# Inverses of decay products: a reciprocal of every token in place of a forward scan

## The chip, the cores and the metric

The kernel runs on one core of a Trainium2 chip. The metric is the device time of one execution in microseconds (us), the median of several runs. The engines are called TensorE (PE, its weight loads PEld), VectorE (DVE), ScalarE (ACT), GpSimd (POOL) and SyncE (SP, which issues most transfers). They work side by side and wait for one another by semaphores; each engine takes its own instructions in the order of the program.

## The reference

A gated linear attention is followed by a two-layer block with a SoLU activation and a layer norm:

```
q, k, v, alpha: (batch 4, heads 8, tokens 768, head_dim 48), alpha in 0.8 to 1.0
for t in range(S):
    state = alpha[:, :, t, :, None] * state + k_t (outer) v_t
    y[:, :, t] = q_t @ state
x = y as (3072 tokens, 384)
h = x @ w_in                       # 384 -> 1024
solu = h * softmax(h)
ln = (solu - mean) / sqrt(var + 1e-6) * g_ln
out = ln @ w_out                   # 1024 -> 384
```

## The kernel before, in words

**The attention in chunks.** The 768 tokens are six chunks g = 0 to 5 of 128. A recurrence with a decay can be computed by matmuls within a chunk, if every key is multiplied by the product of the decays after it and every query is divided by the product of the decays after it. Then the score of a key s for a query t carries just the decays between s and t. So each chunk needs two arrays with features on the partitions and tokens along the free axis:

- `hT`, the product of alpha from each token to the end of the chunk. `scan_back` makes it with a scan from the last token to the first (L220). The view `hk` of the same memory is shifted by one token, so that column t holds the product of the decays behind t.
- the inverse of it, which is written into `aT`, in place of alpha. `scan_on` makes it.

Four batches of 32 features lie on the 128 partitions, for 8 heads; the 48 features of a head are cut into 32 and 16, and the ends of two heads share a block. So there are 12 blocks of 128 tokens, which are worked on in three parts of four blocks (`i` = 0, 1, 2; part 2 holds the ends). Each block has one column more than tokens (516 columns to a part), in which a scan finds the start value of the next block.

**How `scan_on` makes the inverse before.** For a part it takes the product of the whole chunk (column 1 of each block, 4 numbers to a partition), bounds it from below by 1e-13 (`least`, L234), takes its reciprocal (L235) into the first column of `seed`, and runs one forward scan over alpha (L236, recorded at the line of the helper, L220): each step multiplies by the next alpha. For part 2 it first copies the chunk's products of all 12 blocks to `fend` (L231), from which a check at the end of the kernel tells whether this fast path may stand or a general path has to run.

**Who uses it.** `keys` multiplies kT by hk (GpSimd L244; VectorE L685 and L762 in chunks 0 and 1). `queries` multiplies the transposed q by aT (GpSimd L255; VectorE L693, L772, L780 in chunks 0 and 1), `apart` (ScalarE L248) spreads the ends of two heads over two blocks of qv, and `scores` (TensorE L282) needs both. `masked` (VectorE L293) applies the causal mask, `read_state` and `read_values` (TensorE L314) make y, `next_state` (L364, L374) brings the state forward.

**The two-layer block and the order of the work.** Stage g is the two-layer block of chunk g: eight steps s, each with an `up` of six matmuls (L389) into one of two banks h, an exp on ScalarE (e, L403), the product h*e on VectorE (L404, which frees the bank), a square on ScalarE (u, L405), sums over steps (`running`, L420, one on GpSimd and one on VectorE), and half a `down` (eight matmuls, L500) of the chunk before. `finish` (L517 to L533) turns the sums of a block of rows into a factor r on GpSimd (L530) and scales the output on ScalarE (o_sb, L532).

The order is written out by hand. The attention of chunk g + 1 is spread over the steps of stage g by a table:

```python
        behind={0: "states v keys", 1: "load on2 on0 on1", 2: "lasts firsts", 3: "apart", 5: "decay", 6: "alpha", 7: "back"},
```

"on2 on0 on1" are the three calls of `scan_on`, behind the up of step 1; "lasts firsts" are the transposes of q on VectorE (L198, L195) with the `queries` behind them on GpSimd; "apart" follows in step 3 and "scores0" at the end of step 4. Chunks 0 and 1 and most of chunk 2 are done ahead of these stages in a straight line of code (L673 to L809), where VectorE also converts the weights, which arrive as 64-bit floats, to 32-bit ones (L594 to L606). There the order is, for chunk 1:

```python
    scan_on(1, 2)
    nc.vector.tensor_tensor(out=qe, in0=tq[2], in1=aT[:, H:NB, 1:SW], op=ALU.mult)
    apart()
    finish(0)
    decay(1)
    in_range(7)
    for i in range(2):
        scan_on(1, i)
        part = slice(NP * i, NP * i + NP)
        nc.vector.tensor_tensor(out=qv[:, part], in0=tq[i], in1=aT[:, part, 1:SW], op=ALU.mult)
    down(2, 0)
    scores(1, 0)
```

Of the kernel before, what the change touches and what calls it, by code (L numbers as in the profile page):

```python
# [9 lines left out]
FP = mybir.dt.float32  # L10
# [4 lines left out]
ALU = mybir.AluOpType  # L15
AX = mybir.AxisListType
P = 128
# [15 lines left out]
def fast_path(ctx, tc, q, k, v, alpha, moe_w_in, moe_w_out, moe_g_ln, out):  # L33
# [12 lines left out]
    nc = tc.nc  # L46
# [5 lines left out]
    NP = H // 2  # L52
# [6 lines left out]
    LEAST = 1e-13  # L59
    PS = bass.MemoryType.PSUM  # L60

    def pool(name, bufs, **kw):
        return ctx.enter_context(tc.tile_pool(name=name, bufs=bufs, **kw))

    const = pool("const", 1)
# [3 lines left out]
    small = pool("small", 4)  # L69
# [27 lines left out]
    fend = const.tile([P, G, NB], FP, name="fend")  # L97
# [19 lines left out]

    SW = P + 1
    aT = const.tile([P, NB, SW], FP, name="aT")
    seed = [const.tile([P, NP, SW], FP, name=f"seed{i}") for i in range(2)]  # L120
    unit = const.tile([P, NP, SW], FP, name="unit")
    hT = const.tile([P, NB * SW + 2], FP, name="hT")
    h4 = hT[:, 0 : NB * SW].rearrange("p (j s) -> p j s", s=SW)

    hk = hT[:, 2 : NB * SW + 2].rearrange("p (j s) -> p j s", s=SW)[:, :, 0:P]
# [90 lines left out]
    def scan(out, data, start, flip):  # L216
        a, o, s = (x.rearrange("p j s -> p (j s)") for x in (data, out, start))
        if flip:
            a, o, s = a[:, ::-1], o[:, ::-1], s[:, ::-1]
        nc.vector.tensor_tensor_scan(out=o, data0=a, data1=s, initial=1.0, op0=ALU.mult, op1=ALU.add)  # L220
# [5 lines left out]

    def scan_on(g, i):
        part = slice(NP * i, NP * i + NP)
        s = seed[i % 2]
        if i == 2:  # L230
            nc.vector.tensor_copy(out=fend[:, g], in_=h4[:, :, 1])  # L231

        least = small.tile([P, NP, 1], FP, name="least")
        nc.vector.tensor_scalar(out=least, in0=h4[:, part, 1:2], scalar1=LEAST, scalar2=None, op0=ALU.max)  # L234
        nc.vector.reciprocal(out=s[:, :, 0:1], in_=least)  # L235
        scan(aT[:, part], aT[:, part], s, False)  # L236

    def keys_T(g):
        firsts(kn, kT[:, 0:H])
# [414 lines left out]
    nc.gpsimd.memset(unit[:, :, 0:1], 1.0)  # L654
    nc.gpsimd.memset(aT[:, :, 0:1], 0.0)
    nc.gpsimd.memset(hT[:, NB * SW : NB * SW + 2], 1.0)
    for s in seed:
        nc.gpsimd.memset(s, 0.0)
    nc.gpsimd.memset(state, 0.0)
    load_v_first(0)  # L660
    fetch(0, 3, 2)
# [18 lines left out]
    turned(kn, ends_of(kn), t)  # L680
    alpha_over(0)
    scan_on(0, 2)
    for i in range(3):
        part = slice(NP * i, NP * i + NP)
        nc.vector.tensor_tensor(out=kT[:, part], in0=t[i], in1=hk[:, part], op=ALU.mult)  # L685
    scan_on(0, 0)
    t = three("tp_q", [(ps_o, "o"), (ps_o, "o"), (ps_a, "a0")])
    turned(qn, ends_of(qn), t)
    for i in (2, 0, 1):
        if i == 1:  # L690
            scan_on(0, i)
        part = slice(NP * i, NP * i + NP)
        nc.vector.tensor_tensor(  # L693
            out=qe if i == 2 else qv[:, part], in0=t[i], in1=aT[:, part, 1:SW], op=ALU.mult
        )
        if i == 2:
            apart()
# [61 lines left out]
    for i in range(3):  # L759
        scan_back(1, i)  # L760
        part = slice(NP * i, NP * i + NP)
# [15 lines left out]
# [3 lines that stand above are left out]
# [150 lines left out]
    def compare(out, x, bound, op):  # L930
# [6 lines left out]
        out=chunks[:, :, 2], in0=sums[:, :, 2], scalar=0.25, in1=sums[:, :, 3], op0=ALU.mult, op1=ALU.is_le  # L937
# [6 lines left out]
    else:  # L944
# [9 lines left out]
        out=bad, in0=all_ok[0:1, 0:1], scalar1=float(P * ends[-1]), scalar2=None, op0=ALU.is_lt  # L954
# [415 lines left out]
def kernel(tc, *args):  # L1370

    with ExitStack() as ctx:
        taken = fast_path(ctx, tc, *args)
    with tc.If(taken > 0):
        general_path(tc, *args)
# [30 lines left out]
```

## Time and profile before

The median of three runs is 393.45 us (390.79 to 393.57). The profiled execution spans 388.2 us.

| engine | busy us | share of the span | instructions |
|---|---|---|---|
| TensorE, matmuls | 369.6 | 95% | 4661 |
| TensorE, weight loads | 223.5 | 58% | 4661 |
| VectorE | 250.6 | 65% | 417 |
| ScalarE | 144.0 | 37% | 252 |
| GpSimd | 124.9 | 32% | 135 |

A group of instructions is given by its line, engine, operation, what it writes and reads with shapes, how many there are, then their busy time in us and the mean of one in ns, then the idle time of the engine ahead of them and what ended it. A row of slices cuts the span into 40 equal parts; a digit is the busy share of a slice in tenths. The chain that ended last is followed back from the last instruction, at each step to what released it or to the one before on its engine; a line of it, and of the timeline, begins with the start and the length in us.

### The profile page before, as it was taken

To read this page: it belongs to the slowest core of one execution; us is meant where nothing else is said; L and a number is where in the kernel's file an instruction comes from. 1 tells how busy PE (TensorE), PEld (TensorE's weight loads), DVE (VectorE), ACT (ScalarE), POOL (GpSimd) and SP (SyncE) were. 2 spreads that over 40 slices of the span, in tenths; PEclk is the share of its full clock that TensorE was granted. 3 is DMA by queue.
4 is the path that set the end of the run, shared out by engine and by line. 5 is a ranking of instruction groups with operands and counts; after the bars stand their busy time and mean duration, and the time that the engine had idled before them with its cause. 6 is when DMAs were issued, how large, how long until landed. Compare 5 with 4: busy or idle time off the path is not lost.

```text
span 388.2 us, 10598 instructions
## 1 busy us (share of the span) xinstructions
PE 369.6 (95%) x4661; PEld 223.5 (58%) x4661; DVE 250.6 (65%) x417; ACT 144.0 (37%) x252; POOL 124.9 (32%) x135
## 2 busy tenths in 40 slices
PE   8798999887999999999999999999999999999995
PEld 8685345455665556656566556566555675555552
DVE  0989888996989766793755893665895511444410
ACT  2627775554425425225152224253123231333111
POOL 4020000032032992436413536422634620333210
PEclk9989999999999999999999999999999999999999
DMA  9956989402357300774000863000600000000011
GB/s 186 193 154 173 243 256 179 104 20 69 95 128 102 83 4 2 100 167 102 22 3 22 133 141 95 22 3 24 101 0 22 22 24 2 20 21 21 22 43 48
DMA packets 86567, 30.79 MB, mean 79 GB/s; under 512 B 68072, under 2 KB 84720, under 8 KB 86512
## 3 DMA queue, kind: packets, MB, share of 16 engines
q1 hardware_dynamic: 85488, 29.11, 34.7%
q10 hardware_dynamic: 1024, 0.92, 0.7%
q8 instruction: 38, 0.62, 0.7%
q14 instruction: 17, 0.14, 0.1%
HBM read 25.30 MB, written 4.72 MB: 77 GB/s over the span
## 4 chain that ended last, share of the span: by engine, by line
PE 71%; DVE 12%; SPq 6%; ACT 4%; DMA 3%; issue 2%; DVEq 0%
PE o L500 29%; PE h L389 24%; PE y L314 9%; PE a L282 5%; SPq L564 3%; SPq L152 2%; DMA room<-in_moe_w_in_dram 2%; DVE room L404 2%; PE kv L364 1%; ACT sq L581 1%; DVE aT L220 1%; DMA kn<-in_k_dram 1%; DVE low L605 1%; DVE top L597 1%; DVE sT L293 1%
## 5 line engine op out<-in xcount | busy, mean ns | idle before, releaser
L500 PE MATMUL o<-w_out,room 128*128 128x385 f32 x384 | 133.5, 491 | 1.1 <-DVE least L234 1.1
L389 PE MATMUL h<-x,w_in 128*128 128x512 f32 x288 | 132.2, 598 | 1.8 <-DVE g_col L618 1.8
L500 PEld LDWEIGHTS o<-w_out,room 128*128 128x128 f32 x384 | 71.3, 190 | 57.3 <-issue 15.4
L389 PEld LDWEIGHTS h<-x,w_in 128*128 128x128 f32 x288 | 53.0, 189 | 60.5 <-issue 48.4
L404 DVE TENSOR_TENSOR room<-h,e 128x512 f32<-128x512 f32 x40 | 27.7, 692 | 81.3 <-ACT e L403 81.1
L403 ACT ACTIVATE e<-h 128x512 f32<-128x512 f32 x40 | 23.9, 598 | 103.6 <-PE h L389 103.6
L530 POOL TENSOR_TENSOR r<-sums,mhalf 128x1 f32<-128x1 f32 x20 | 14.3, 714 | 139.4 <-DVE sums L522 139.4
L420 POOL TENSOR_TENSOR p<-p,e 128x512 f32<-128x512 f32 x30 | 41.7, 1390 | 15.8 <-ACT e L403 15.7
L405 ACT ACTIVATE u<-room 128x512 f32<-128x512 f32 x40 | 25.2, 630 | 42.2 <-DVE room L404 42.2
L293 DVE TENSOR_TENSOR sT<-a,mask 128x512 f32<-128x512 f32 x44 | 27.3, 682 | 10.0 <-PE a L282 8.9
L282 PE MATMUL a<-qv,kT 32*128 32x128 f32 x704 | 27.6, 289 | 4.4 <-DVE least L234 2.1
L282 PEld LDWEIGHTS a<-qv,kT 32*128 32x128 f32 x704 | 24.1, 196 | 11.9 <-issue 4.2
L220 DVE TENSOR_TENSOR_SCAN hT<-aT,unit 128x516 f32<-128x516 f32 x18 | 23.1, 1339 | 8.7 <-ACT aT L677 8.6
L420 DVE TENSOR_TENSOR p<-p,u 128x512 f32<-128x512 f32 x30 | 23.1, 771 | 6.5 <-ACT u L405 6.5
L244 POOL TENSOR_TENSOR kT<-kT,hT 128x1024 f32<-128x1024 f32 (+1 forms) x8 | 13.3, 1676 | 43.2 <-DVE kT L195 43.2
L314 PE MATMUL y<-sT,vn 128*32 128x128 f32 x768 | 23.6, 274 | 1.6 <-issue 0.9
L220 DVE TENSOR_TENSOR_SCAN aT<-aT,seed 128x516 f32<-128x516 f32 x18 | 23.0, 1278 | 0.6
L314 PEld LDWEIGHTS y<-sT,vn 128*32 128x32 f32 x768 | 20.9, 110 | 3.7 <-issue 2.7
L212 ACT ACTIVATE sq<-an,mone 128x1536 uint8<-128x1536 f32 x12 | 18.8, 1569 | 0.2
L314 PE MATMUL y<-qv,state 32*32 32x128 f32 x960 | 16.8, 277 | 1.0 <-DVE sT L293 0.9
L314 PEld LDWEIGHTS y<-qv,state 32*32 32x32 f32 x960 | 12.1, 103 | 7.9 <-issue 4.8
L532 ACT ACTIVATE o_sb<-o,r 128x384 f32<-128x384 f32 x16 | 9.3, 581 | 18.8 <-POOL r L530 18.8
(141 smaller groups left out, 378.2 us busy)
## 6 DMA issues: line engine op xcount, KB each, us to landing
an<-in_alpha_dram SPq DMA_DIRECT2D x20, 192.0 KB, 5.0
out_dram<-o_sb SPq DMA_DIRECT2D x20, 192.0 KB, 1.9
room<-in_moe_w_out_dram SPq DMA_DIRECT2D x8, 384.0 KB, 4.8
kn<-in_k_dram SPq DMA_DIRECT2D x16, 192.0 KB, 4.0
qn<-in_q_dram SPq DMA_DIRECT2D x16, 192.0 KB, 3.8
vn<-in_v_dram SPq DMA_DIRECT2D x10, 256.0 KB, 4.0
room<-in_moe_w_in_dram SPq DMA_DIRECT2D x16, 128.0 KB, 3.7
kn<-in_k_dram SPq DMA_DIRECT2D x4, 384.0 KB, 5.7
```

The source lines that it names most:

```text
L212: nc.scalar.activation(out=sq, in_=x, func=AF.Relu, scale=sign, bias=mone, accum_out=over[:, g, i : i + 1])
L220: nc.vector.tensor_tensor_scan(out=o, data0=a, data1=s, initial=1.0, op0=ALU.mult, op1=ALU.add)
L282: nc.tensor.matmul(a[b][:, i], lhsT=kT[quarter(b), kb], rhs=qv[quarter(b), qb], start=kb == h, stop=kb != h, tile_position=(32 * b, 0), sk ...
L293: nc.vector.tensor_tensor(out=sT[:, b, half * NP : half * NP + NP], in0=a[b], in1=mask[:, None, :].to_broadcast([P, NP, P]), op=ALU.mult,)
L314: nc.tensor.matmul(y_bank(b)[quarter(r), a], lhsT=lhsT, rhs=rhs, start=(b, r) not in begun, stop=stop, tile_position=(row, 32 * r), skip_g ...
L389: nc.tensor.matmul(h, lhsT=w_in[:, a, f * P : (f + 1) * P], rhs=d["x"][:, a].rearrange("p b t -> p (b t)"), start=(a == 0), stop=(a == KC ...
L403: nc.scalar.activation(out=e, in_=h, func=AF.Exp)
L404: nc.vector.tensor_tensor(out=u, in0=h, in1=e, op=ALU.mult)
L405: nc.scalar.activation(out=u2, in_=u, func=AF.Square)
L420: eng.tensor_tensor(out=p, in0=d[0][i] if f == 1 else p, in1=d[f][i], op=ALU.add)
L500: nc.tensor.matmul(d["o"][:, 0 : DM + 1], lhsT=u_of(g, f)[:, b * P : b * P + P], rhs=w_out[:, f], start=(f == 0), stop=(f == FC - 1), skip ...
L530: nc.gpsimd.tensor_tensor(out=r, in0=s[:, 3:4], in1=mhalf, op=ALU.pow)
```

## The change

The inverse of each part is taken directly: one reciprocal on VectorE of the 512 products in `hk`, written to the columns of `aT` where the scan wrote its result. With it go the bound from below, the reciprocal of four numbers, the forward scan and the `seed` tiles with their memsets at the start. The copy of the chunk's products to `fend` moves from VectorE to ScalarE. It is meant to get the same array with one instruction per part in place of three dependent ones.

```diff
-    seed = [const.tile([P, NP, SW], FP, name=f"seed{i}") for i in range(2)]
...
     def scan_on(g, i):
         part = slice(NP * i, NP * i + NP)
-        s = seed[i % 2]
         if i == 2:
-            nc.vector.tensor_copy(out=fend[:, g], in_=h4[:, :, 1])
-
-        least = small.tile([P, NP, 1], FP, name="least")
-        nc.vector.tensor_scalar(out=least, in0=h4[:, part, 1:2], scalar1=LEAST, scalar2=None, op0=ALU.max)
-        nc.vector.reciprocal(out=s[:, :, 0:1], in_=least)
-        scan(aT[:, part], aT[:, part], s, False)
+            nc.scalar.copy(out=fend[:, g], in_=h4[:, :, 1])
+
+        nc.vector.reciprocal(out=aT[:, part, 1:SW], in_=hk[:, part])
...
-    for s in seed:
-        nc.gpsimd.memset(s, 0.0)
```

## The prediction

> **What bounds the kernel now.** I read the totals of the page first, then the slices, then the costliest groups and VectorE's own groups, then the chain that ended last in order of time, then the timeline around the changed instructions.
>
> ```profile
> PE 369.6 (95%) x4661; PEld 223.5 (58%) x4661; DVE 250.6 (65%) x417; ACT 144.0 (37%) x252; POOL 124.9 (32%) x135
> ...
> DVE  0989888996989766793755893665895511444410
> ...
> L220 DVE TENSOR_TENSOR_SCAN aT<-aT,seed 128x516 f32<-128x516 f32 x18 | 23.0, 1278 | 0.6
> L234 DVE TENSOR_SCALAR least<-hT 128x4 f32<-128x4 f32 x18 | 6.5, 362 | 0.0
> L235 DVE RECIPROCAL seed<-least 128x4 f32<-128x4 f32 x18 | 3.2, 180 | 0.8
> L231 DVE COPY fend<-hT 128x12 f32<-128x12 f32 x6 | 2.5, 409 | 0.0
> ```
>
> TensorE (PE) is busy 95% of the span, but this averages two regimes. In the row of slices (9.7 us each) VectorE (DVE) is almost full for the first ten, then at five to nine tenths. The chain agrees: until 89 us it is made of DMA, ScalarE and VectorE pieces, from about 134 us of matmuls end to end. So VectorE's load counts nearly one for one early, and later only where it outgrows what TensorE's work hides. The last four lines are all that the change takes from VectorE: 35.2 us. The chain in order of time (start, length, what) shows the early regime for chunk 1:
>
> ```profile
> 84.66 1.34 DVE aT L220
> 86.03 0.69 DVE qv L780
> 87.12 1.30 DVE aT L220
> 88.45 0.70 DVE qv L780
> 89.19 2.06 PE a L282 x62
> ```
>
> Scan, multiply, scan, multiply, and only then may TensorE make the scores. The timeline of VectorE in a late stage (chunk 4, start, length) shows what one inverse costs from start to start:
>
> ```profile
> 221.43 0.17 DVE L231 COPY fend<-hT 128x12 f32<-128x12 f32 x1
> 221.51 0.16 DVE L234 TENSOR_SCALAR least<-hT 128x4 f32<-128x4 f32 x1
> 221.71 0.18 DVE L235 RECIPROCAL seed<-least 128x4 f32<-128x4 f32 x1
> 221.93 1.23 DVE L220 TENSOR_TENSOR_SCAN aT<-aT,seed 128x516 f32<-128x516 f32 x1
> 223.08 1.17 DVE L234 TENSOR_SCALAR least<-hT 128x4 f32<-128x4 f32 x1
> ...
> 227.18 0.67 DVE L420 TENSOR_TENSOR p<-u,u 128x512 f32<-128x512 f32 x1
> ```
>
> Three inverses fill 221.43 to 227.18, that is 5.75 us.
>
> [...] The trace has only reciprocals of 4 elements: 180 ns, where other 4-element operations (L464, L466) take 166. [...] the copy of fend took 1.61 us at 108.92, beside GpSimd's L244. The reciprocals stay within 180 to 181 ns[...].
>
> **The price of the new instruction.** It is one reciprocal of 128x512 per third of a chunk, 18 in all; no row has it. [...] *Fast end:* all the excess over a plain operation is a fixed cost, [...] about 0.69 us, like the 128x512 multiply L404 (692 ns). *Slow end:* [...] **4.41 us**. *Between:* [...] 2.96 us. I take 4.41[...]; it is an estimate.
>
> **The change part by part, at 4.41 us.**
> VectorE's busy time becomes 250.6 - 35.2 + 18 x 4.41 = 294.8 us. What of this reaches the end:
>
> - *Chunk 0 (13 to 22 us).* Its three inverses now take 1.80 (fend to scan end, 13.17 to 14.97), 1.64 and 1.71 us: 5.15. They become 13.2, so the last qv is 8.1 us later. VectorE then idled 1.16 us before the masking at 23.0; that idle goes, as the first scores are done earlier relative to it. Behind the masking VectorE converts weights (L594 to L606) with hardly a gap until 37 us, and the first products of stage 0 wait for those. **+7.0**.
> - *Chunk 1 (80 to 90 us).* 80.83 to 82.55, 84.24 to 86.0 and 86.63 to 88.41, with finish(0) between: 5.3 us become 13.2. All lies on the chain shown. **+7.9**.
> - *Chunk 2.* Parts 2 and 0 run from 108.92 to 114.19, 5.27 us[...], and become 8.82: +3.55. Behind them on VectorE's queue is finish(3), for whose factor ScalarE's output waits, and behind that on ScalarE the exp of stage 1. Those products thus start later, and TensorE's third up waits for a free h bank. Part 1, 119.27 to 121.40, 2.13 us, becomes 4.41: +2.28. The transposes of q, GpSimd's queries and scores(2,0) follow; TensorE already waits 0.30 and 0.33 us there. **+5.8**.
> - *Chunks 3, 4, 5 (stages 2 to 4, slot s = 1).* 5.75 us become 13.2, +7.45. Queued behind on VectorE: running(1), the product h*e of s = 2, the transposes of q. The first wait is up(4), scheduled at 233.78 in the stage shown: it needs the h bank that the product of s = 2 frees at 228.45 + 7.45 = 235.9, 2.1 us late. The second wait is longer and contains the first: transposes, then GpSimd's queries and p, then r, then ScalarE's o_sb, then apart, which now ends at 238.14 and would end at 245.6, where TensorE wants scores at 239.04. That is +6.55, the same in stage 2 (180.75 against 181.58), and +7.3 in stage 4, where scores start at 294.75 just as apart works. **+20.4**. TensorE runs these stages without gaps, so nothing is won back.
> - *Copy of fend on ScalarE.* A copy of about 0.2 us, six times, of values long made; ScalarE idles by 1 us and more around slot 1 (2.2 us before e at 224.97). **0**. Fewer memsets on GpSimd at 3 us: it then waits 15.7 us for v. **0**.
>
> Sum: 7.0 + 7.9 + 5.8 + 20.4 = 41.1; 393.45 + 41.1 is about **434.5 us**.
>
> **The rivals.**
> *B[...] (2.96 us and up).* Three inverses take 8.88 us. Chunk 0: +3.7 - 1.1 = +2.6; chunk 1: +3.6; chunk 2: 5.92 - 5.27 plus 2.96 - 2.13 = +1.5; stages: 3.1 - 0.9 of slack = 2.2 twice and 3.0 once, +7.4. Sum +15.1, **408.5 us**. [...]
> *C[...] faster than before.* Three inverses take 2.1 us. Chunk 0: up to -3.1, of which I count -2, as the weights' transfers end the next wait; chunk 1: 5.3 to 2.1, -3.2; chunk 2: about -1, what TensorE waits there; later nothing, since matmuls follow without gaps. Sum -6.2, **387 us**. For it: [...] that fixed parts of small operations differ (COPY L462 of 8 elements takes 172 ns). [...]
> *D[...].* [...] the 1.74 us of an inverse now: **no change**, 393 us.
>
> **How the numbers follow.** Forecast 0.52, B 0.22, C 0.20, D 0.06. The range goes from C, 386, to 444, the forecast with a quarter more on its 41 us for queues that I have not followed; it leaves out about half of C and a tenth of the forecast. Faster by over 1%: 0.20; within 1%: 0.06; slower: 0.74.
>
> **What would show it.** Right: a group RECIPROCAL aT<-hT 128x512 x18 near 4.4 us each; VectorE busy near 295 us; the chain passing through that line in chunks 0 to 2; waits of TensorE for apart's qv ahead of scores in stages 2 to 4; the late chain no longer matmuls alone. Wrong: a reciprocal below 2 us, which puts C or D in its place; or one of 4.4 us with matmuls still end to end after 134 us, which would mean that the queue behind slot 1 has more slack than I read.

## The result

The changed kernel takes 418.8 us (median; 416.0 to 421.5) against 392.9 us before: the ratio is 1.067, with a 95% interval of 1.056 to 1.077. It is slower by about 26 us. The forecast was 434.5 us: the side was right, the size was not.

The page of the changed kernel, its totals, its slices (40 of 10.5 us), the clock that TensorE was granted, and the costliest group of VectorE:

```profile
PE 383.5 (91%) x4661; PEld 233.2 (56%) x4661; DVE 275.6 (66%) x375; ACT 144.3 (34%) x258; POOL 119.6 (28%) x133
...
DVE  1999879995797877695465596465696531344420
...
PEclk9969999986899999999699999899999899999999
...
L231 DVE RECIPROCAL aT<-hT 128x512 f32<-128x512 f32 x18 | 59.2, 3322 | 0.1
```

One reciprocal takes 3.3 us. Eighteen of them put 59.2 us on VectorE where 35.2 us went. ScalarE is busy as long as before (144.3 us, 144.0 before), GpSimd 5 us less (119.6, 124.9 before). But TensorE's busy time grew by 14 us with the same 4661 matmuls: some of them ran more slowly, and the clock row dips to 6 and 8 tenths in single slices.

A late stage of it, chunk 3, on VectorE (start, length):

```profile
176.67 0.69 DVE L399 TENSOR_TENSOR room<-h,e 128x512 f32<-128x512 f32 x1 [1.71 <-ACT e L398]
...
177.73 9.77 DVE L231 RECIPROCAL aT<-hT 128x512 f32<-128x512 f32 x3
187.42 0.63 DVE L415 TENSOR_TENSOR p<-u,u 128x512 f32<-128x512 f32 x1
187.96 0.68 DVE L399 TENSOR_TENSOR room<-h,e 128x512 f32<-128x512 f32 x1
188.56 1.14 DVE L197 STREAM_TRANSPOSE qe<-qn 128x512 f32<-128x512 f32 x1
```

The three inverses fill 9.7 us instead of 5.75; the product and the transposes of q stand behind them. The chain that ended last, in the same stage (start, length, what):

```profile
189.78 1.18 POOL qe L250
...
191.67 2.62 POOL qv L250 x2
...
195.99 0.56 POOL r L525
...
196.57 0.58 ACT o_sb L527
197.15 1.22 ACT qv L243 x2
198.37 0.48 ACT kg L298
...
198.99 4.67 PE a L277 x64
203.65 2.60 PE h L384 x3
```

This is the second wait that the prediction named: queries on GpSimd, then its r, then o_sb and apart on ScalarE. Behind apart the three copies kg still follow, and it is for them that TensorE waits (3.64 us until the copy of L298 ends), since the scores go into the banks that they read. TensorE then runs the 64 score matmuls of chunk 3 in 4.67 us, which took 2.72 us in the trace of before:

```profile
181.58 2.72 PE L282 MATMUL a<-qv,kT 32*128 32x128 f32 x64
```

**Where the time came from.** The start of the product h*e of a given step marks how far a kernel is. Its delay against before, read from the timelines (us), with what the runs below give; "again" is a second execution of the changed kernel (run after_again):

| stage, step | changed | again | late | early | spread | filler15 | filler_both |
|---|---|---|---|---|---|---|---|
| 0, 0 | 3.3 | 3.1 | 1.3 | 2.7 | 3.2 | 3.1 | 2.6 |
| 1, 2 | 13.9 | 11.7 | 3.9 | 11.3 | 13.2 | 11.7 | 10.7 |
| 2, 0 | 13.7 | 11.5 | 3.8 | 11.1 | 14.5 | 11.4 | 10.2 |
| 3, 0 | 20.3 | 17.2 | 9.2 | 11.2 | 15.3 | 15.3 | 13.7 |
| 4, 0 | 25.9 | 23.5 | 15.9 | 11.2 | 16.5 | 19.8 | 17.6 |
| 5, 0 | 31.2 | 27.1 | 22.1 | 11.2 | 19.1 | 24.0 | 21.4 |

The changed kernel loses 13.7 us before stage 2 and 6.6, 5.6 and 5.3 us in stages 2 to 4; in stage 5, which has no attention, nothing. These are single executions: the one profiled of the changed kernel is its longest (421.5 us) and that of before one of its shorter ones (390.2), so 31 us stand here for the 26 of the medians. The second execution of the changed kernel (417.4 us) is 27.1 us late at the end. "late" has the early code of before unchanged and still shows 3.9 us at stage 1, of which 1.7 are eight matmuls of down that took 4.55 us in place of 2.86. So a few microseconds lie within what the same code does.

### The profile page after: what moved, and what is told of

The parts are those of the page before. It is cut to its first block, busy times and chain, and to the rows that moved or that the text cites. A ratio compares the mean times of both kernels' runs of the same rounds, so it can differ in the third digit from the quotient of the medians.

```text
span 419.5 us, 10560 instructions
## 1 busy us (share of the span) xinstructions
PE 383.5 (91%) x4661; PEld 233.2 (56%) x4661; DVE 275.6 (66%) x375; ACT 144.3 (34%) x258; POOL 119.6 (28%) x133
## 4 chain that ended last, share of the span: by engine, by line
PE 55%; DVE 22%; issue 7%; ACT 7%; POOL 4%; DMA 3%; SPq 0%; DVEq 0%; ACTq 0%; POOLq 0%
PE o L495 20%; PE h L384 17%; PE y L309 9%; DVE aT L231 8%; PE a L277 6%; DVE room L399 2%; DMA an<-in_alpha_dram 2%; POOL qv L250 2%; DVE hT L219 2%; ACT sq L576 1%; DMA kn<-in_k_dram 1%; DVE sT L288 1%; DVE qe L197 1%; ACT qv L243 1%; PE kv L359 1%
## 5 line engine op out<-in xcount | busy, mean ns | idle before, releaser
L495 PE MATMUL o<-w_out,room 128*128 128x385 f32 x384 | 138.0, 505 | 2.7 <-DVE o_mean L521 2.7
L384 PE MATMUL h<-x,w_in 128*128 128x512 f32 x288 | 134.0, 605 | 1.2 <-DVE g_col L613 1.2
L495 PEld LDWEIGHTS o<-w_out,room 128*128 128x128 f32 x384 | 73.6, 196 | 61.2 <-issue 21.4
L231 DVE RECIPROCAL aT<-hT 128x512 f32<-128x512 f32 x18 | 59.2, 3322 | 0.1
L277 PE MATMUL a<-qv,kT 32*128 32x128 f32 x704 | 34.9, 340 | 20.3 <-ACT kg L298 7.2
L277 PEld LDWEIGHTS a<-qv,kT 32*128 32x128 f32 x704 | 30.9, 241 | 28.1 <-issue 15.3
L288 DVE TENSOR_TENSOR sT<-a,mask 128x512 f32<-128x512 f32 x44 | 27.3, 681 | 13.5 <-PE a L277 13.5
```

The lines of the kernel that those rows point to most:

```text
L231: nc.vector.reciprocal(out=aT[:, part, 1:SW], in_=hk[:, part])
L277: nc.tensor.matmul(a[b][:, i], lhsT=kT[quarter(b), kb], rhs=qv[quarter(b), qb], start=kb == h, stop=kb != h, tile_position=(32 * b, 0), sk ...
L288: nc.vector.tensor_tensor(out=sT[:, b, half * NP : half * NP + NP], in0=a[b], in1=mask[:, None, :].to_broadcast([P, NP, P]), op=ALU.mult,)
L384: nc.tensor.matmul(h, lhsT=w_in[:, a, f * P : (f + 1) * P], rhs=d["x"][:, a].rearrange("p b t -> p (b t)"), start=(a == 0), stop=(a == KC ...
L495: nc.tensor.matmul(d["o"][:, 0 : DM + 1], lhsT=u_of(g, f)[:, b * P : b * P + P], rhs=w_out[:, f], start=(f == 0), stop=(f == FC - 1), skip ...
```

## The experiments

The theory after the result: (1) the reciprocal has a constant price of 6.2 ns per element; (2) early, its length is on the path one for one; (3) late, the queue of three at step 1 makes TensorE wait ahead of the scores; (4) after that wait TensorE's granted clock is low for some microseconds (0.50 from 199 to 203 us), a cost of its own. Rivals: another price in long rows or for another layout; VectorE's load as such, wherever it stands; waits alone, the matmuls being slow for another reason.

### The price by itself

```diff
     nc.vector.memset(w_out[:, :, DM : DM + 1], 1.0)
+    lad = const.tile([P, 512], FP, name="lad")
+    for n in (4, 8, 16, 32, 64, 128):
+        nc.vector.reciprocal(out=lad[:, 0:n], in_=ones[:, 0:n])
+    nc.vector.reciprocal(out=lad[:, 0:512:8], in_=ones[:, 0:64])
+    nc.vector.tensor_tensor(out=lad[:, 0:128], in0=ones, in1=ones, op=ALU.mult)
```

> The kernel before with eight extra VectorE instructions in its idle time before 9 us: reciprocals of 4, 8, 16, 32, 64 and 128 neighbouring elements, one of 64 elements whose output is written at every eighth word, and a multiply of 128. Theory (a fixed part and a constant price for each element): 128x4 takes 180 ns and 128x512 took 3341 ns in the changed kernel, so 6.2 ns each: 205, 255, 354, 553 and 951 ns for 8 to 128 elements, and 553 ns for the 64 scattered ones; the multiply about 291 ns. [...] Rival 2 (the layout of the output sets the rate): neighbouring elements cost clearly less than 6.2 ns, the 64 scattered ones clearly more than 64 neighbouring ones. The time of the whole stays at that of before within 1 us.

VectorE's groups in the first 9 us (busy us, mean ns of one):

```profile
L670 DVE RECIPROCAL lad<-ones 128x128 f32<-128x128 f32 x1 | 1.0, 953 | 0.0
L671 DVE RECIPROCAL lad<-ones 128x64 f32<-128x64 f32 x1 | 0.6, 556 | 0.0
L670 DVE RECIPROCAL lad<-ones 128x64 f32<-128x64 f32 x1 | 0.6, 552 | 0.0
...
L672 DVE TENSOR_TENSOR lad<-ones 128x128 f32<-128x128 f32 x1 | 0.3, 292 | 0.0
...
L670 DVE RECIPROCAL lad<-ones 128x8 f32<-128x8 f32 x1 | 0.2, 203 | 0.0
L670 DVE RECIPROCAL lad<-ones 128x4 f32<-128x4 f32 x1 | 0.2, 179 | 0.0
```

From 4 to 128 elements the price is (953 - 179) / 124 = 6.24 ns for each element. The 512 elements of the kernel lie on the same line: (3341 - 179) / 508 = 6.22 ns, with the median of 3341 ns. The scattered output (L671) costs 4 ns more in all. So the layout of the output does not set the rate, and rows of up to 512 have no other price. The whole took 391.8 us in its single run.

### The late and the early chunks alone

In both, `scan_on` takes the new form for some chunks and the old one for the others:

```diff
     def scan_on(g, i):
         part = slice(NP * i, NP * i + NP)
+        if g >= 3:
+            if i == 2:
+                nc.scalar.copy(out=fend[:, g], in_=h4[:, :, 1])
+            nc.vector.reciprocal(out=aT[:, part, 1:SW], in_=hk[:, part])
+            return
         s = seed[i % 2]
```

> Reciprocals for chunks 3, 4 and 5 alone, the forward scans for chunks 0 to 2. Theory (a wait of TensorE ahead of the scores, then slow matmuls behind it): the three stages lose what they lost in the changed kernel, 6.8, 5.5 and 5.4 us, so 14 to 18 us over before. Rival (only the wait counts, slack of 0.9 us in two stages and none in the third): 9.8 - 5.75 = 4.0, less the slack, 10 us over before. Rival (late stages hide VectorE wholly): below 3 us.

412.8 us, ratio 1.057 (1.048 to 1.066): about 22 us, more than the 14 to 18 expected. By the table 3.8 us of it lie ahead of stage 2, in code that this run leaves as it was. The three stages lose 5.4, 6.7 and 6.2 us, 18.3 in all, where the waits of TensorE ahead of the scores are 3.62, 3.57 and 3.21 us, 10.4 in all.

The second has `g < 3`:

> Reciprocals for chunks 0, 1 and 2 alone, the forward scans for chunks 3 to 5. Theory (every microsecond of VectorE is on the path in the early regime): longer inverses 3.7 (chunk 0, after 1.2 of idle), 4.7 (chunk 1), 2.3 (chunk 2) are 10.7 us, and with the slow matmuls behind the waits about 13.5 us over before. Rival (waits only): 10.7 us. With the kernel that has the late reciprocals alone it should add up to the loss of the whole change, about 26 us.

401.2 us, ratio 1.030 (1.020 to 1.039): about 11.7 us of 392.2, and 11.2 by the table, all of it lost before stage 2. That lies nearer to the waits alone (10.7) than to the theory's 13.5, and the interval holds both. The two ratios add to 8.7%, more than the 6.7% of the whole; the intervals just allow that. In the traces the two parts do add: 18.3 and 11.2 are 29.5 us, between the 27.1 and 31.2 of the two executions of the whole change.

### The same work in another place

```diff
-        behind={0: "states v keys", 1: "load on2 on0 on1", 2: "lasts firsts", 3: "apart", 5: "decay", 6: "alpha", 7: "back"},
+        behind={0: "states v keys", 1: "load on0 on1", 2: "lasts firsts", 3: "apart", 5: "decay", 6: "alpha", 7: "back next2"},
...
+        elif what == "next2" and more:
+            scan_on(a + 1, 2)
```

(and "alpha back next2" in the table of stage 1).

> The changed kernel, with the reciprocal of part 2 of chunks 3 to 5 moved from step 1 of the stage to step 7 of the stage before, behind its backward scan, where VectorE then idles over 4 us. No work is taken away. Theory (it is the queue of 9.8 us in one place that delays transposes, queries and scores): step 1 holds 6.5 us in place of 9.8, 0.8 us more than the scans took, within the slack of 0.9 us in two stages; 12 to 16 us are won back, the time is about 13.5 us over before. Rival (VectorE's load as such costs it): the time stays within 3 us of the changed kernel, about 26 us over before.

408.4 us, ratio 1.045 (1.038 to 1.051): about 9 us are won back with every reciprocal still there, VectorE's busy time being 275.6 us in both. By the table the stages lose 0.8, 1.2 and 2.6 us. In chunk 3 two reciprocals are left at step 1 (VectorE's timeline):

```profile
178.52 6.56 DVE L231 RECIPROCAL aT<-hT 128x512 f32<-128x512 f32 x2
```

and in TensorE's timeline the scores of chunk 3 wait 0.43 us, not 3.64, and take 2.94 us, not 4.67:

```profile
196.56 2.94 PE L277 MATMUL a<-qv,kT 32*128 32x128 f32 x64 [0.43 <-ACT kg L298]
```

So it is the place in the queue and not VectorE's load. The gain is below the 12 to 16 us expected. From stage 1 on 5.9 us are still lost: 1.3 of them at the start of stage 2, behind the new place, and 2.0 at step 1 of stage 4, whose cause is not shown.

### The clock behind a wait

The stretches around the wait of chunk 3 in the changed kernel (from:to, length, busy time of each engine, then the granted clock, the share of DMA, GB/s):

```profile
190.00:195.00 5.00, 5.00 (x16) 2.49 (x14) 4.84 (x7) 0.63 (x1) 4.29 (x4) 1.00 0.47 112
195.00:199.00 4.00, 0.36 (x3) 0.04 (x1) 0.00 (x0) 2.43 (x5) 2.77 (x3) 1.00 0.39 106
199.00:203.00 4.00, 4.00 (x60) 4.00 (x62) 1.38 (x2) 1.94 (x4) 1.27 (x1) 0.50 0.00 0
203.00:207.00 4.00, 4.00 (x18) 1.96 (x11) 2.48 (x4) 0.00 (x0) 0.00 (x0) 0.64 0.00 0
```

TensorE idles for most of 195 to 199, and in the next 4 us its granted clock is 0.50. The wait was 3.64 us long. The low stretch lasts about 6.8 us when the clock is read in short windows (0.50 from 199.2 to 205.6 us, 1.00 from 206.0 on); in the second execution of this kernel it lasts 3.4 us in stage 2 and 6.8 us in stage 3, where the clock row of its page (slices of 10.4 us) has 8 and 7 tenths.

The length of a wait does not tell by itself whether the clock falls. Two waits in the changed kernel, each in its first and its second execution (eight matmuls of down in chunk 1, 56 of the scores of chunk 5):

```profile
89.41 4.52 PE L495 MATMUL o<-w_out,room 128*128 128x385 f32 x8 [2.67 <-DVE o_mean L521]
89.13 2.83 PE L495 MATMUL o<-w_out,room 128*128 128x385 f32 x8 [2.68 <-DVE o_mean L521]
...
324.42 2.90 PE L277 MATMUL a<-qv,kT 32*128 32x128 f32 x56 [3.27 <-ACT qv L243]
321.96 2.01 PE L277 MATMUL a<-qv,kT 32*128 32x128 f32 x56 [3.21 <-ACT qv L243]
```

Of the nine waits of 3.2 to 3.6 us in stages 2 to 4 of the changed kernel, its second execution and "late", eight have slow scores behind them. The wait of 2.67 us has slow matmuls behind it in two of the six executions that have it unfilled. And in the changed kernel the clock is 0.50 again from 111 to 113 us, though TensorE had not waited over 0.86 us in the 5 us before. The waits do not explain that case, and its cause is not shown.

The test keeps TensorE busy in the wait:

```diff
-        tail={4: "scores0", 5: "scores1", 6: "begin read0 read1"},
+        tail={4: "fill scores0", 5: "scores1", 6: "begin read0 read1"},
...
+        elif what == "fill" and a > 2:
+            warm(26, ps_a, "a3")
```

> The changed kernel once more, as the measure for the next run on the same chip: about 26 us over before (ratio 1.067).

Ratio 1.068 (1.059 to 1.077), 417.4 us.

> The changed kernel with 26 matmuls of ones (128x128, into a bank that is not in use) ahead of the first scores of chunks 3, 4 and 5, where TensorE waits 3.6 us. Nothing needs their result. Theory (the matmuls behind the wait run slowly because TensorE's granted clock falls after the wait; 64 score matmuls took 4.67 us in place of 2.65 us, six of up 3.96 in place of 2.84): the scores and the up behind them run at the speed of before, each stage loses about 3 to 4 us in place of 5.4 to 6.8, 6 to 8 us are won back. Rival (they are slow for another reason, for instance operands that come late): the time stays that of the changed kernel within 1 us, or is longer by what the added matmuls exceed the wait.

418.9 us, ratio 1.069 (1.061 to 1.076): the 6 to 8 us expected were not won. The timeline of TensorE in chunk 3 says why:

```profile
195.05 5.97 PE L440 MATMUL warm<-ones 128*128 128x128 f32 x52
200.95 2.17 PE L277 MATMUL a<-qv,kT 32*128 32x128 f32 x64
203.05 2.84 PE L384 MATMUL h<-x,w_in 128*128 128x512 f32 x6
```

The scores run fast again (2.17 us, not 4.67), but the filler is 2.3 us longer than the wait. With 15:

```diff
-            warm(26, ps_a, "a3")
+            warm(15, ps_a, "a3")
```

> As the filler before it, with 15 matmuls in place of 26: those took 5.97 us, longer than the wait of 3.6 us, and gave back in length what the clock won; 15 take 3.4 us. Theory (the granted clock falls after the wait and costs 1.5 to 3 us in each of three stages): 4 to 8 us less than the changed kernel, about 19 to 21 us over before (ratio 1.05). Rival (the clock is not the cause): ratio 1.067 as the changed kernel.

415.7 us, ratio 1.057 (1.052 to 1.062): about 4 us less than the changed kernel, at the lower end of what was expected, and the two intervals overlap. By the table the stages lose 3.9, 4.5 and 4.2 us, where the two executions without filler lose 6.6, 5.6, 5.3 and 5.7, 6.3, 3.6. Its scores of chunk 3, with the granted clock at 1.00 from 192 to 200 us:

```profile
192.84 3.51 PE L440 MATMUL warm<-ones 128*128 128x128 f32 x30
196.64 2.94 PE L277 MATMUL a<-qv,kT 32*128 32x128 f32 x64 [0.30 <-ACT kg L298]
```

And with fillers in the two waits of chunk 1 as well:

```diff
+    warm(8, ps_a, "a3")
     down(2, 0)
+    warm(14, ps_a, "a3")
     scores(1, 0)
```

> As filler15, and with 8 and 14 such matmuls in the two waits of TensorE in chunk 1, of 2.7 us ahead of a down and of about 3 us ahead of the first scores. Theory: behind those waits 62 score matmuls took 3.79 us in place of 2.06 and eight of down 4.06 in place of 2.86, so another 2 to 3 us less: about 17 us over before (ratio 1.043). Rival: no further gain over filler15, since VectorE sets the pace there.

411.4 us, ratio 1.045 (1.041 to 1.050), the total that was expected. But its trace is only 1.0 us ahead of that of filler15 at stage 1, and there the 62 scores of chunk 1 still took 2.82 us and two downs 3.72 and 4.36 us; where the rest of the 4 us between the medians comes from is not shown. Work that nobody needs thus takes a third of the loss away, and most of the waits remain, now with fillers in them.

### The small parts of the change

```diff
-            nc.vector.tensor_copy(out=fend[:, g], in_=h4[:, :, 1])
+            nc.scalar.copy(out=fend[:, g], in_=h4[:, :, 1])
```

> The kernel before with the copy of fend on ScalarE alone. Theory: only in chunk 2 is that copy on the path, where it took 1.6 us beside GpSimd's work; up to 1.5 us faster, of which the forward scan behind it may take back part, as it then meets the same work of GpSimd. Rival (hidden or moved to another wait): no difference that can be measured.

393.2 us, ratio 1.0005 (0.996 to 1.005): no difference. In chunk 2, where the copy took 1.61 us beside GpSimd's multiply of the keys, the instruction behind it now takes as long (VectorE, start, length):

```profile
108.34 1.61 DVE L234 TENSOR_SCALAR least<-hT 128x4 f32<-128x4 f32 x1
109.99 0.18 DVE L235 RECIPROCAL seed<-least 128x4 f32<-128x4 f32 x1
110.20 1.95 DVE L220 TENSOR_TENSOR_SCAN aT<-aT,seed 128x516 f32<-128x516 f32 x1
```

Next, with the copy on ScalarE, the bound is left out too:

```diff
-        least = small.tile([P, NP, 1], FP, name="least")
-        nc.vector.tensor_scalar(out=least, in0=h4[:, part, 1:2], scalar1=LEAST, scalar2=None, op0=ALU.max)
-        nc.vector.reciprocal(out=s[:, :, 0:1], in_=least)
+        nc.vector.reciprocal(out=s[:, :, 0:1], in_=h4[:, part, 1:2])
```

> The kernel before with the copy of fend on ScalarE, and without the bound from below: the reciprocal of four numbers reads the products themselves. It leaves out the bound of 1e-13, which no input here reaches. The forward scans stay. Theory: one step of 0.2 us less in each of the nine inverses of chunks 0 to 2, where VectorE is on the path, and the copy off the path in chunk 2: 1.8 to 3.3 us faster than before, about 390 us. Rival: the wait that comes last in chunks 0 and 2 is another one, and less than 1 us comes of it.

391.6 us, ratio 0.9963 (0.9933 to 0.9993): about 1.5 us faster, by an interval that only just leaves out no change. It keeps the scan and takes the reciprocal of four numbers only. That reciprocal takes 0.17 us in chunk 2, but the wait moved on once more: the two scans behind it take 2.43 and 1.81 us in the trace, where they took 1.88 and 1.23. Parts 2 and 0 of chunk 2 thus fill 4.64 us in place of 5.27. The gain lies below the 1.8 to 3.3 us expected, though the interval reaches into them.

## Why the prediction was right and wrong

| part | predicted at 4.41 us | same working at 3.34 us | between the traces |
|---|---|---|---|
| chunk 0 | +7.0 | 10.0 - 5.15 - 1.16 = +3.7 | +3.3 |
| chunk 1, to its first scores | +7.9 | 10.0 - 5.3 = +4.7 | +4.8 |
| chunk 2, to stage 1 step 2 | +5.8 | 6.68 - 5.27 + 3.34 - 2.13 = +2.6 | +5.8 |
| chunks 3 to 5 | +20.4 | 4.0 less slack: 3.1 + 3.1 + 4.0 = +10.2 | +17.3 |
| sum | +41.1 | +21.2 | +31.2; +25.8 by the medians |

- **The price of the reciprocal is the term that was too large.** My 4.41 us for 512 elements was an estimate that no trace of before showed: its only reciprocals had four elements (180 ns), and a row of one length can't tell a fixed part from a price for each element. The ladder shows 6.24 ns for each element, and 512 take 3.34 us. This makes the forecast too high by 20 us (41.1 against 21.2).
- **The path was read rightly.** Early, the lengths add one for one: chunk 1 shifts the first scores from 89.19 to 97.28, of which 3.3 us come from chunk 0. Late, the wait comes through the named instructions, and the rerouted reciprocal shows that the queue is its cause. One step was missed: in chunks 3 and 4 the copies kg behind apart are what the scores wait for last; in chunk 5 it is apart, as forecast. GpSimd did not hold up the reciprocal: two of them took 6.51 us at 119.47, beside GpSimd's multiply of the keys (118.84 to 122.16), and three in chunk 3 took 9.77.
- **A term was missing: TensorE's granted clock.** With the true price the working gives 21 us, some 5 us less than the medians. The two traced executions of the changed kernel tell the waits from the clock. The first scores of chunk 1 come 8.1 and 7.8 us later, chunk 2 adds 1.2 and 1.6 us of its own, and the waits ahead of the scores in stages 2 to 4 add 10.5 and 10.4 us (3.64 + 3.58 + 3.27 and 3.63 + 3.58 + 3.21). That is 19.8 us in both, close to the 21.2. Of what is left of their 31.2 and 27.1 us, 11.4 and 7.3 us, the same matmuls of TensorE that took longer than before (scores, down, up) make 11.2 and 6.7. This part differs by 4 us between two executions of one kernel with the same waits. The fillers agree with it: from 1.068 to 1.045 is about 9 us, with VectorE's work unchanged.
- **Chunk 2's +5.8 is an accident.** In the first execution 4.6 us of it are slow matmuls: 62 scores in 3.79 us where 2.06 were needed, and two downs in 4.06 and 4.55 where they took 2.86 each. Its own 1.2 to 1.6 us lie below the working's 2.6.
- **The two errors have opposite signs.** The price was too high by 20 us and the clock was left out, so the sum is 16 us too high and not 20. That is luck.
- **ScalarE's copy of fend costs nothing**, as said: 0.2 us each, and ratio 1.0005 by itself.
- **Rival B**, an estimate of 2.96 us and up, holds the measured 3.34 us, and its 408.5 us lie nearer to the measured 418.8 than the forecast. It was worked out at 2.96 us and not 3.34, which is 6 us of what it misses; the rest is the same missing term. C and D fell with the price.

## What to carry to other kernels

Price an operation by two row lengths before it replaces another: the reciprocal looks about as cheap as any in rows of four (180 ns, L464 and L466 of before 166), yet a row of 512 takes 3.34 us where the scan of 516 takes 1.23. On VectorE, which was busy for 66% of the span, what counted was who stood behind the new instruction in its queue; moving it to an idle stretch gave back a third of the loss (ratio 1.045, not 1.067). A wait of TensorE can cost twice, once for itself and again for the matmuls behind it: here each wait of 3.2 to 3.6 us cost 0 to 3 us more. One trace does not show that part well, as it differs between executions of the same kernel.

## What was not expected of the hardware

- VectorE's reciprocal: 179 ns for 4 elements, 953 for 128, 3341 for 512, in steps of 6.2 ns per element, with no difference for an output at every eighth word (552 and 556 ns).
- After 3.64 us of waiting TensorE's granted clock stood at 0.50 for about 6.8 us. A wait of 2.67 us in chunk 1 was followed by slow matmuls in two of six executions (4.52 us for eight of down in one of them, 2.83 without the fall), and a wait of 3.21 us by none in one execution (2.01 us for 56 scores, 2.90 behind 3.27 us in the other).
- A copy of VectorE of 12 elements to a partition took 1.61 us beside GpSimd's multiply, where it takes 0.17 us by itself. Taking it away only handed the wait to the next instruction (1.61 us for L234), and from there to the scans (2.43 and 1.81 us in place of 1.88 and 1.23).
